# Small tiles moved and padded so that every matmul operand in SBUF begins at a multiple of 512 bytes

## The chip, the core and the metric

The kernel runs on one core of one Trainium2 chip. The metric is the device time of one execution in microseconds (us), as the median of several runs. The profile is of one further execution. TensorE is the matmul engine, VectorE, ScalarE and GpSimd are the others; in the profile they are PE (PEld for its weight loads), DVE, ACT and POOL. SBUF is the on-chip memory: 128 partitions, and a tile has the same address range in each of them. An address below is the byte offset in a partition.

## What is computed

Linear attention with a decaying state for 4 batches, 8 heads, 768 steps and head size 64, and behind it two MLPs over the 3072 tokens:

```python
state = gamma * state + k[t] (outer) v[t];  y[t] = scale * q[t] @ state     # per batch and head
h = x @ w_in;  solu = h * softmax(h);  ln = (solu - mu) / sqrt(var + 1e-6) * g_ln
x = ln @ w_out                                # first MLP, 512 -> 1024 -> 512
h = x @ w_in2;  g = h * cos(h);  out = g @ w_out2       # second MLP, 512 -> 2048 -> 512
```

## The kernel before

**Precision.** Each operand of the MLP matmuls is split in a high and a low half (`split`, line 119: ScalarE writes the high half, VectorE the rest), and each product is three matmuls: high by high, high by low, low by high. Before each matmul TensorE loads its stationary operand (`lhsT`, 128x128); the moving operand (`rhs`) then streams through, 512 columns or, in `mm2`, 256.

**Stages.** The order of TensorE's work is the program's own (a manual schedule); the other engines follow an order that the framework plans from it. Up to about 110 us attention steps, the first MLP and the loading of weights start up. Up to about 380 us 24 attention steps (`att_scores`, `att_state`, `att_out`) alternate with the first MLP: `mm1` (line 284) multiplies 128 tokens by `w_in`, `norm` (line 292 to 305) does the softmax and the normalization with a small tile `sm` of row statistics, `transp` (line 320) transposes, and `mm2` (line 337) multiplies by `w_out`. Then the second MLP goes over six blocks of 512 tokens. Its weights `w2h`, `w2l` are in four chunks of 512 hidden units. For each of 16 groups j of 128 hidden units `up` (line 362) makes 12 matmuls with chunk j // 4; ScalarE and VectorE form h cos(h) (line 369 to 374: a range reduction and a sine with the bias tile `hp`, which holds pi/2, then `split`), and `down` (line 387), three groups later, makes 12 matmuls with `o2h`, `o2l`. So `up` and `down` alternate every 12 matmuls, except that at the beginning of each block after the first the four `up` with chunk 0 follow one another, and at the end of a block 48 of `down` do.

**Where the tiles lie.** SBUF pools grow from two sides: "left" from the low addresses and "right" from the high ones. On the left come, in order: 16,384 bytes for DMA and four constants of 32 bytes each (the program's own, up to 16,512), then `mg` (2048), `cs` (576), `gcol` (32), `mhalf` (4, rounded to 32), `ident` (512), the weights of the first MLP, `u`, `x32`, `xh`, `xl`; then three buffers of `sm` (40 bytes, rounded to 64, each), `junk`, `ys`, and behind them `o1h`, `o1l` and the transposed tiles. On the right, from 229,344 downwards: `w2l`, `w2h` of chunk 0, the staging tiles, and the pool of the attention or, later, of the second MLP, at whose low end `hp` lies (4 bytes, rounded to 32, at 151,488) and above it `yh` at 151,520. Where matmuls are concerned this gives, with every slice that a matmul takes a multiple of 512 bytes from the start of its tile:

| operands | side | start of the first tile | remainder modulo 512 |
|---|---|---|---|
| `ident`, `u` (transposes) | left | 19,200 and 52,480 | 256 |
| `w1h`, `w1l` (moving in `mm1`) | left | 19,712 | 256 |
| `xh`, `xl` (stationary in `mm1`) | left | 89,344 | 256 |
| `o1h`, `o1l` (stationary in `mm2`) | left | 101,824 | 448 |
| `lth`, `ltl` (moving in `mm2`) | left | 134,592 | 448 |
| `w2h`, `w2l`, chunk 0 (stationary in `up`) | right | 212,960 | 480 |
| `w2h`, `w2l`, chunks 1 to 3 (stationary in `up`) | left | 19,712 and 85,248 | 256 |
| `yh`, `yl` (moving in `up`) | right | 151,520 | 480 |
| `gh`, `gl` (stationary in `down`) | right | 180,192 | 480 |
| `o2h`, `o2l` (moving in `down`) | left | 52,480 | 256 |
| tiles of the attention (`X`, `kt`, `W`, `kn`) | right | 157,664 | 480 |

Of the kernel before, what the change touches and what calls it, by code (L numbers as in the profile page):

```python
# [11 lines left out]
F32 = mybir.dt.float32  # L12
# [3 lines left out]
AF = mybir.ActivationFunctionType  # L16
# [28 lines left out]
HALFPI = math.pi / 2.0  # L45
# [5 lines left out]
def body(ctx: ExitStack, tc: tile.TileContext, qx, kt, kn, vn, c_sc, c_mg,  # L51
         w_in1, w_out1, gln, w_in2, w_out2, out):
    nc = tc.nc
# [2 lines left out]

    const = ctx.enter_context(tc.tile_pool(name="const", bufs=1, side="left"))
    dram = ctx.enter_context(tc.tile_pool(name="dram", bufs=1, space=DRAM))
    p_w2a = ctx.enter_context(tc.tile_pool(name="w2a", bufs=1, side="right"))
    stg = ctx.enter_context(tc.tile_pool(name="stg", bufs=2, side="right"))  # L60

# [6 lines left out]
    moe = ph1.enter_context(tc.tile_pool(name="moe", bufs=1, side="left", reuse_waits="tile"))  # L68
# [12 lines left out]
    def load_step(n):  # L81
        bp, i = steps[n]
        d = {}
        d["kt"] = pa.tile([128, 8, C], F32, tag="kt", name="kt", bufs=2)
        d["X"] = pa.tile([128, 2, 8, C], F32, tag="X", name="X")
        d["kn"] = pa.tile([128, NHP, 2 * D], F32, tag="kn", name="kn")
        d["W"] = pa.tile([128, 2, 8, D], F32, tag="W", name="W")
        d["mg"] = pa.tile([128, 2, NHP, C], F32, tag="mg", name="mg", bufs=2)
        nc.sync.dma_start(out=d["kt"], in_=kt[bp, i].rearrange("p (j s) -> p j s", s=C))
        src = qx[bp, i].rearrange("p (j s) -> p j s", s=C)  # L90
        nc.sync.dma_start(out=d["X"][64:128, 0], in_=src[64:128])
        nc.sync.dma_start(out=d["X"][0:64, 1], in_=src[0:64])
        src = vn[bp, i].rearrange("p (j s) -> p j s", s=D)
        nc.sync.dma_start(out=d["W"][0:64, 0], in_=src[0:64])
        nc.sync.dma_start(out=d["W"][64:128, 1], in_=src[64:128])
        nc.sync.dma_start(out=d["kn"], in_=kn[bp, i].rearrange("p (j s) -> p j s", s=2 * D))
        if i == 0:
            nc.gpsimd.memset(d["W"][64:128, 0], 0.0)
            nc.gpsimd.memset(d["W"][0:64, 1], 0.0)
        st[n] = d  # L100
# [7 lines left out]
    nc.scalar.dma_start(out=gcol, in_=gln)  # L108
    mhalf = const.tile([128, 1], F32, name="mhalf")
    nc.gpsimd.memset(mhalf, -0.5)  # L110
    ident = const.tile([128, 128], F32, name="ident")
    make_identity(nc, ident)

# [5 lines left out]
    def split(hi, lo, src, pin=False, head=None):  # L119
        op = nc.scalar.activation(out=hi, in_=src if head is None else head, func=AF.Copy)  # L120
        if pin:
            tc.keep_in_program_order(op)
        nc.vector.tensor_tensor(out=lo, in0=src, in1=hi.bitcast(F32), op=ALU.subtract)  # L123

    p2 = {}
# [85 lines left out]
    def att_prep(n):  # L211
        bp, i = steps[n]
        d = st[n]
        nc.gpsimd.tensor_tensor(out=d["mg"], in0=mg, in1=cs[:, 0:2, i].unsqueeze(3).to_broadcast([128, 2, NHP, C]),
                                op=ALU.mult)
        if i + 1 < NI:
            for a in range(NHP):
                nc.scalar.activation(out=d["kn"][:, a], in_=d["kn"][:, a], func=AF.Copy, scale=cs[:, 2, i, a:a + 1])  # L218
# [13 lines left out]
    def att_state(n):  # L232
        bp, i = steps[n]
        if i + 1 >= NI:
            return
        d, nd = st[n], st[n + 1]
        if i == 0:
            s_ps[0] = psa.tile([128, 8, D], F32, tag="S", name="S")
        sp = s_ps[0]
        k3 = d["kn"].rearrange("p a (b d) -> p (a b) d", b=2)  # L240
        for j in range(8):
            nc.tensor.matmul(out=sp[64:128, j], lhsT=k3[0:64, j], rhs=d["W"][0:64, 0, j],  # L242
                             start=(i == 0 and j == 0), stop=(i == NI - 2 and j == 7), skip_group_check=True)
            nc.tensor.matmul(out=sp[0:64, j], lhsT=k3[64:128, j], rhs=d["W"][64:128, 1, j],  # L244
                             start=(i == 0 and j == 0), stop=(i == NI - 2 and j == 7), skip_group_check=True)
        nc.scalar.activation(out=nd["W"][64:128, 0], in_=sp[64:128], func=AF.Copy)
        nc.scalar.activation(out=nd["W"][0:64, 1], in_=sp[0:64], func=AF.Copy)
# [38 lines left out]

    def norm(n):
        h = hs.pop(n)
        sm = moe.tile([128, 10], F32, tag="sm", name="sm", bufs=3)
        junk = moe.tile([128, 2, 512], BF16, tag="junk", name="junk")  # L290
        u = p_u.tile([128, 2, 512], F32, tag="u", name="u")
        nc.vector.tensor_reduce(out=sm[:, 0:1], in_=h, axis=AX.XY, op=ALU.max, negate=True)
        nc.scalar.activation(out=u, in_=h, func=AF.Exp, bias=sm[:, 0:1], accum_out=sm[:, 1:2])
        nc.vector.scalar_tensor_tensor(out=u, in0=u, scalar=1.0, in1=h, op0=ALU.mult, op1=ALU.mult,
                                       accum_out=sm[:, 2:3])
        nc.vector.tensor_scalar(out=sm[:, 3:4], in0=sm[:, 2:3], scalar1=-1.0 / FF1, scalar2=None, op0=ALU.mult)
        nc.scalar.activation(out=junk, in_=u, func=AF.Square, bias=sm[:, 3:4], accum_out=sm[:, 4:5])
        nc.vector.tensor_scalar(out=sm[:, 5:6], in0=sm[:, 1:2], scalar1=1e-9, scalar2=None, op0=ALU.add)
        nc.vector.scalar_tensor_tensor(out=sm[:, 6:7], in0=sm[:, 5:6], scalar=1e-6, in1=sm[:, 5:6],
                                       op0=ALU.mult, op1=ALU.mult)  # L300
        nc.vector.scalar_tensor_tensor(out=sm[:, 7:8], in0=sm[:, 4:5], scalar=1.0 / FF1, in1=sm[:, 6:7],
                                       op0=ALU.mult, op1=ALU.add)
        nc.gpsimd.tensor_tensor(out=sm[:, 8:9], in0=sm[:, 7:8], in1=mhalf, op=ALU.pow)
        nc.vector.tensor_tensor(out=sm[:, 9:10], in0=sm[:, 3:4], in1=sm[:, 8:9], op=ALU.mult)
        nc.scalar.activation(out=u, in_=u, func=AF.Identity, scale=sm[:, 8:9], bias=sm[:, 9:10])
        lns[n] = u
# [47 lines left out]
    def up(n, j):  # L354
        yh, yl = p2["y", n]
        wh, wl = w2h[j // 4], w2l[j // 4]
        cs = slice((j % 4) * 128, (j % 4) * 128 + 128)
        h = p2["psh"].tile([128, 512], F32, tag="h2", name="h2")
        m = 0
        for k in range(KD):  # L360
            for w, a in ((wh, yh), (wl, yh), (wh, yl)):
                nc.tensor.matmul(out=h, lhsT=w[:, k, cs], rhs=a[:, k], start=(m == 0), stop=(m == 3 * KD - 1))  # L362
                m += 1
        sb = p2["sb"]
        ki = sb.tile([128, 512], I32, tag="ki", name="ki", bufs=2)
        r = sb.tile([128, 512], F32, tag="r", name="r", bufs=2)
        gh = sb.tile([128, 512], F32R, tag="gh", name="gh", bufs=LAG + 1)
        gl = sb.tile([128, 512], F32R, tag="gl", name="gl", bufs=LAG + 1)
        nc.scalar.activation(out=ki, in_=h, func=AF.Identity, scale=INV2PI, bias=0.25)  # L369
        nc.vector.scalar_tensor_tensor(out=r, in0=ki, scalar=-C1, in1=h, op0=ALU.mult, op1=ALU.add)  # L370
        nc.vector.scalar_tensor_tensor(out=r, in0=ki, scalar=-C2, in1=r, op0=ALU.mult, op1=ALU.add)
        nc.vector.tensor_scalar(out=r, in0=r, scalar1=HI, scalar2=LO, op0=ALU.min, op1=ALU.max)  # L372
        nc.scalar.activation(out=r, in_=r, func=AF.Sin, bias=p2["hp"])  # L373
        nc.vector.tensor_tensor(out=r, in0=r, in1=h, op=ALU.mult)  # L374
        split(gh, gl, r)
        p2["g", n, j] = (gh, gl)
# [49 lines left out]
    def attend():  # L426
        n = nxt[0]
        if n >= ns:
            return
        nxt[0] += 1  # L430
        if 4 < n + 2 < ns:
            load_step(n + 2)
        if n == 0:
            att_state(n)
            att_out(n)
        if n + 1 < ns:
            att_prep(n + 1)
            att_scores(n + 1)
        if n > 0:
            att_state(n)  # L440
            att_out(n)
        if n == ns - 1:
            att.close()
            p2["psh"] = ctx.enter_context(tc.tile_pool(name="psh", bufs=3, side="right", space=PSUM, reuse_waits="tile"))
            p2["sb"] = ctx.enter_context(tc.tile_pool(name="sb2", bufs=1, side="right", reuse_waits="tile"))
            p2["hp"] = p2["sb"].tile([128, 1], F32, name="hp")
            nc.gpsimd.memset(p2["hp"], HALFPI)

    def first(n, c):
        if c == 1 and 0 < n < 2 * NG - 1:  # L450
# [183 lines left out]
```

## Time and profile before

| | |
|---|---|
| median of 3 runs | 952.97 us (952.46 to 953.57) |
| the profiled execution | 950.22 us |
| its span, first to last instruction | 948.4 us |
| TensorE matmuls busy | 917.0 us (97%) |
| TensorE weight loads busy | 776.5 us (82%) |
| VectorE, ScalarE, GpSimd busy | 622.4, 452.8, 47.8 us |

The span is what the trace covers; the time of an execution has 1.8 us around it. Matmuls are pipelined: the recorded length of one overlaps the next, so busy time says only that TensorE had work. How fast that goes is seen from the starts in the timeline, or from the chain of waits, in which each piece of several instructions stands with its length.

### The profile page before, as it was taken

Reading aid. Unit: us, or ns where it says so; the run is one execution under the profiler, and the core shown is the slowest. Engines: PE = TensorE matmul, PEld = TensorE weight load, DVE = VectorE, ACT = ScalarE, POOL = GpSimd, SP = SyncE. Lnnn points to the kernel's source line nnn. Section 1 sums busy time; section 2 is a strip of 40 time slices with the busy share of each in tenths; the row PEclk is TensorE's granted clock in tenths of the full one; section 3 lists DMA queues with packets and bytes.
Section 4 is the critical chain, followed back from the end, with each engine's and each line's share of the span. In section 5 each row is a group of like instructions: output and inputs, shape, how many; then the busy total and the mean of one; then the engine's idle time right before and its main releaser. Section 6 shows DMA issues by size and latency. Waiting matters only on the chain.

```text
span 948.4 us, 16045 instructions
## 1 busy us (share of the span) xinstructions
PE 917.0 (97%) x6464; PEld 776.5 (82%) x6464; DVE 622.4 (66%) x1090; ACT 452.8 (48%) x768; POOL 47.8 (5%) x60
## 2 busy tenths in 40 slices
PE   4887999999999999999999999999999999999997
PEld 4676899899898999998888888888888888888886
DVE  5899887668677664566657555755665566556553
ACT  4677756565655544644434333433433343334332
POOL 2112110110101100000000000000000000000000
PEclk9999999999999999999999999999999999999999
DMA  9997355656456332242011003000300020001001
GB/s 257 283 257 201 113 153 170 197 168 216 154 170 204 105 101 67 83 145 73 1 53 37 0 1 90 1 1 0 89 1 1 23 66 1 1 23 45 0 1 45
DMA packets 41882, 85.26 MB, mean 90 GB/s; under 512 B 5456, under 2 KB 11728, under 8 KB 41808
## 3 DMA queue, kind: packets, MB, share of 16 engines
q1 hardware_dynamic: 41376, 83.91, 29.9%
q8 instruction: 50, 0.82, 0.4%
q10 hardware_dynamic: 432, 0.34, 0.1%
q14 instruction: 24, 0.20, 0.1%
HBM read 64.30 MB, written 19.92 MB: 89 GB/s over the span
## 4 chain that ended last, share of the span: by engine, by line
PE 90%; DMA 4%; DVE 2%; ACT 2%; issue 1%; SPq 0%; POOL 0%; ACTq 0%; DVEq 0%
PE acc L387 28%; PE h L362 28%; PE y L337 14%; PE h L284 11%; DMA kn<-kn_dram 3%; PE tr L320 2%; PE y L256 2%; PE sc L224 2%; PE S L244 1%; DMA W<-vn_dram 1%; DVE X L227 1%; ACT kn L218 1%; DMA mg<-c_mg_dram 0%; PE S L242 0%; PE sc L225 0%
## 5 line engine op out<-in xcount | busy, mean ns | idle before, releaser
L387 PE MATMUL acc<-o2h,gl 128*128 128x512 f32 x384 | 151.9, 396 | 0.0
L387 PE MATMUL acc<-o2l,gh 128*128 128x512 f32 x384 | 151.8, 395 | 0.0
L362 PE MATMUL h<-yh,w2h 128*128 128x512 f32 x384 | 151.8, 395 | 0.0
L362 PE MATMUL h<-yl,w2h 128*128 128x512 f32 x384 | 151.5, 395 | 0.0
L362 PE MATMUL h<-yh,w2l 128*128 128x512 f32 x384 | 151.5, 395 | 0.0
L387 PE MATMUL acc<-o2h,gh 128*128 128x512 f32 x384 | 151.5, 395 | 0.0
L373 ACT ACTIVATE r<-r,hp 128x512 f32<-128x512 f32 x96 | 69.3, 722 | 144.9 <-DVE r L372 144.6
L370 DVE SCALAR_TENSOR_TENSOR r<-ki,h 128x512 f32<-128x512 int32 x96 | 66.0, 687 | 73.7 <-ACT ki L369 72.6
L337 PE MATMUL y<-lth,o1h 128*128 128x256 f32 x384 | 110.4, 287 | 0.0
L337 PE MATMUL y<-ltl,o1h 128*128 128x256 f32 x384 | 108.9, 284 | 0.0
L337 PE MATMUL y<-lth,o1l 128*128 128x256 f32 x384 | 108.7, 283 | 0.0
L374 DVE TENSOR_TENSOR r<-r,h 128x512 f32<-128x512 f32 x96 | 66.0, 688 | 61.6 <-ACT r L373 61.6
L369 ACT ACTIVATE ki<-h 128x512 int32<-128x512 f32 x96 | 57.2, 596 | 85.6 <-PE h L362 84.8
L123 DVE TENSOR_TENSOR gl<-r,gh 128x512 fp32r<-128x512 f32 x96 | 66.3, 691 | 45.9 <-ACT gh L120 45.4
L120 ACT ACTIVATE gh<-r 128x512 fp32r<-128x512 f32 x96 | 60.6, 632 | 65.0 <-DVE r L374 64.9
L387 PEld LDWEIGHTS acc<-o2h,gl 128*128 128x128 f32 x384 | 72.1, 188 | 17.7
L387 PEld LDWEIGHTS acc<-o2h,gh 128*128 128x128 f32 x384 | 72.0, 188 | 17.4
L387 PEld LDWEIGHTS acc<-o2l,gh 128*128 128x128 f32 x384 | 72.1, 188 | 17.2
L362 PEld LDWEIGHTS h<-yl,w2h 128*128 128x128 f32 x384 | 72.2, 188 | 17.0
L362 PEld LDWEIGHTS h<-yh,w2h 128*128 128x128 f32 x384 | 72.2, 188 | 16.9
L362 PEld LDWEIGHTS h<-yh,w2l 128*128 128x128 f32 x384 | 72.2, 188 | 16.6
L284 PE MATMUL h<-w1h,xh 128*128 128x512 f32 x192 | 77.8, 405 | 0.0
(79 smaller groups left out, 1597.3 us busy)
## 6 DMA issues: line engine op xcount, KB each, us to landing
raw<-w_in_dram SPq DMA_DIRECT2D x24, 512.0 KB, 4.6
raw<-w_out_dram SPq DMA_DIRECT2D x24, 512.0 KB, 4.4
kt<-kt_dram SPq DMA_DIRECT2D x24, 256.0 KB, 4.6
X<-qx_dram SPq DMA_DIRECT2D x48, 128.0 KB, 4.9
W<-vn_dram SPq DMA_DIRECT2D x48, 128.0 KB, 4.5
kn<-kn_dram SPq DMA_DIRECT2D x24, 256.0 KB, 4.8
y1d<-ys SPq DMA_DIRECT2D x24, 256.0 KB, 2.2
yt<-y1d SPq DMA_DIRECT2D x24, 256.0 KB, 3.0
```

What stands on the lines that cost most here:

```text
L120: op = nc.scalar.activation(out=hi, in_=src if head is None else head, func=AF.Copy)
L123: nc.vector.tensor_tensor(out=lo, in0=src, in1=hi.bitcast(F32), op=ALU.subtract)
L224: nc.tensor.matmul(out=sc[0:64, j], lhsT=d["kt"][64:128, j], rhs=d["X"][64:128, 0, j], start=True, stop=True)
L256: nc.tensor.matmul(out=y[64 * par:64 * par + 64, j], lhsT=d["W"][:, par, j], rhs=d["X"][:, par, j], start=True, stop=True)
L284: nc.tensor.matmul(out=h[:, c], lhsT=a[:, k], rhs=w[:, k, cs], start=(k + m == 0), stop=(k == KD - 1 and m == 2))
L337: nc.tensor.matmul(out=y1[:, e], lhsT=w[:, j, ds], rhs=a[:, j % 2], start=(m == 0), stop=(m == 3 * K1 - 1))
L362: nc.tensor.matmul(out=h, lhsT=w[:, k, cs], rhs=a[:, k], start=(m == 0), stop=(m == 3 * KD - 1))
L369: nc.scalar.activation(out=ki, in_=h, func=AF.Identity, scale=INV2PI, bias=0.25)
L370: nc.vector.scalar_tensor_tensor(out=r, in0=ki, scalar=-C1, in1=h, op0=ALU.mult, op1=ALU.add)
L373: nc.scalar.activation(out=r, in_=r, func=AF.Sin, bias=p2["hp"])
L374: nc.vector.tensor_tensor(out=r, in0=r, in1=h, op=ALU.mult)
L387: nc.tensor.matmul(out=acc, lhsT=a[:, ts_], rhs=w, start=(j == 0 and m == 0), stop=(j == K2 - 1 and m == 2))
```

## The change

A new pool on the right, opened before all others of that side, holds `hp` as a tile of 480 bytes, of which the first element is set to pi/2 at the start of the program and read by the sine; before, `hp` was a tile of 4 bytes in the pool of the second MLP, set when the attention was done. The row statistics `sm` are now three tiles of 64 bytes among the constants on the left, taken in turn by `n % 3`, ahead of `ident`, with a `pad` of 64 bytes behind them; before, they were three buffers of a pool, behind `xl`. No arithmetic and no instruction on data changes, and no operand changes its side.

```diff
--- before.py
+++ after.py
@@ -56,6 +56,8 @@
 
     const = ctx.enter_context(tc.tile_pool(name="const", bufs=1, side="left"))
     dram = ctx.enter_context(tc.tile_pool(name="dram", bufs=1, space=DRAM))
+    p_hp = ctx.enter_context(tc.tile_pool(name="hp", bufs=1, side="right"))
+    hp = p_hp.tile([128, 120], F32, name="hp")
     p_w2a = ctx.enter_context(tc.tile_pool(name="w2a", bufs=1, side="right"))
     stg = ctx.enter_context(tc.tile_pool(name="stg", bufs=2, side="right"))
 
@@ -108,6 +110,9 @@
     nc.scalar.dma_start(out=gcol, in_=gln)
     mhalf = const.tile([128, 1], F32, name="mhalf")
     nc.gpsimd.memset(mhalf, -0.5)
+    nc.gpsimd.memset(hp[:, 0:1], HALFPI)
+    sms = [const.tile([128, 16], F32, name=f"sm{n}") for n in range(3)]
+    const.tile([128, 16], F32, name="pad")
     ident = const.tile([128, 128], F32, name="ident")
     make_identity(nc, ident)
 
@@ -286,7 +291,7 @@
 
     def norm(n):
         h = hs.pop(n)
-        sm = moe.tile([128, 10], F32, tag="sm", name="sm", bufs=3)
+        sm = sms[n % 3]
         junk = moe.tile([128, 2, 512], BF16, tag="junk", name="junk")
         u = p_u.tile([128, 2, 512], F32, tag="u", name="u")
         nc.vector.tensor_reduce(out=sm[:, 0:1], in_=h, axis=AX.XY, op=ALU.max, negate=True)
@@ -370,7 +375,7 @@
         nc.vector.scalar_tensor_tensor(out=r, in0=ki, scalar=-C1, in1=h, op0=ALU.mult, op1=ALU.add)
         nc.vector.scalar_tensor_tensor(out=r, in0=ki, scalar=-C2, in1=r, op0=ALU.mult, op1=ALU.add)
         nc.vector.tensor_scalar(out=r, in0=r, scalar1=HI, scalar2=LO, op0=ALU.min, op1=ALU.max)
-        nc.scalar.activation(out=r, in_=r, func=AF.Sin, bias=p2["hp"])
+        nc.scalar.activation(out=r, in_=r, func=AF.Sin, bias=hp[:, 0:1])
         nc.vector.tensor_tensor(out=r, in0=r, in1=h, op=ALU.mult)
         split(gh, gl, r)
         p2["g", n, j] = (gh, gl)
@@ -443,8 +448,6 @@
             att.close()
             p2["psh"] = ctx.enter_context(tc.tile_pool(name="psh", bufs=3, side="right", space=PSUM, reuse_waits="tile"))
             p2["sb"] = ctx.enter_context(tc.tile_pool(name="sb2", bufs=1, side="right", reuse_waits="tile"))
-            p2["hp"] = p2["sb"].tile([128, 1], F32, name="hp")
-            nc.gpsimd.memset(p2["hp"], HALFPI)
 
     def first(n, c):
         if c == 1 and 0 < n < 2 * NG - 1:
```

## Rows read from the trace of the kernel before

**Rows 1.** The profile's page: part 1, busy time of the engines.

```profile
PE 917.0 (97%) x6464; PEld 776.5 (82%) x6464; DVE 622.4 (66%) x1090; ACT 452.8 (48%) x768; POOL 47.8 (5%) x60
```

**Rows 2.** The cores: span and mean granted TensorE clock.

```profile
core 0: 948.4 us, clock 0.993
```

**Rows 3.** Windows by stage; the first line names the columns.

```profile
core 0: us, PE busy (x) PEld busy (x) DVE busy (x) ACT busy (x) POOL busy (x), PEclk, DMA share, GB/s
0.00:25.00 25.00, 12.60 (x193) 11.41 (x194) 14.65 (x25) 10.90 (x23) 5.10 (x12) 1.00 0.91 262
25.00:50.00 25.00, 19.03 (x292) 15.61 (x290) 20.56 (x35) 14.38 (x31) 2.45 (x2) 0.93 1.03 290
...
240.00:380.00 140.00, 139.81 (x1316) 126.65 (x1315) 90.04 (x184) 75.55 (x125) 11.10 (x15) 1.00 0.41 132
490.00:580.00 90.00, 90.00 (x389) 72.69 (x388) 54.53 (x89) 35.46 (x58) 0.00 (x0) 1.00 0.09 24
```

**Rows 4.** TensorE's waits, the longest: total us, times, longest one.

```profile
PE sc L224 <- DMA X<-qx_dram: 11.1, 2, 5.7
```

**Rows 5.** The chain of waits, second MLP: start us, length us, what.

```profile
485.87 11.20 PE acc L387 x48
497.07 10.92 PE h L362 x48
...
516.38 2.80 PE h L362 x12
```

**Rows 6.** Timeline of TensorE, `up` with chunk 0: matmuls 1, 10; then `down`.

```profile
496.90 0.40 PE L362 MATMUL h<-yh,w2h 128*128 128x512 f32 x1
...
498.98 0.39 PE L362 MATMUL h<-yh,w2h 128*128 128x512 f32 x1
...
507.82 0.40 PE L387 MATMUL acc<-o2h,gh 128*128 128x512 f32 x1
```

**Rows 7.** Timeline of TensorE, `mm1` after `mm2`: matmuls 1, 10, 24.

```profile
110.53 0.39 PE L284 MATMUL h<-w1h,xh 128*128 128x512 f32 x1
...
112.62 0.39 PE L284 MATMUL h<-w1h,xh 128*128 128x512 f32 x1
...
115.79 0.39 PE L284 MATMUL h<-w1l,xh 128*128 128x512 f32 x1
```

**Rows 8.** Timeline, matmul and next weight load: `down`, then `up` with chunk 0.

```profile
486.17 0.40 PE L387 MATMUL acc<-o2l,gh 128*128 128x512 f32 x1
486.18 0.19 PEld L387 LDWEIGHTS acc<-o2h,gh 128*128 128x128 f32 x1
...
500.34 0.39 PE L362 MATMUL h<-yh,w2h 128*128 128x512 f32 x1
500.35 0.19 PEld L362 LDWEIGHTS h<-yh,w2l 128*128 128x128 f32 x1
```

**Rows 9.** Timeline of TensorE, `down` after `mm2`: matmuls 1, 3, 10, 12.

```profile
418.53 0.39 PE L387 MATMUL acc<-o2h,gh 128*128 128x512 f32 x1
...
418.98 0.39 PE L387 MATMUL acc<-o2l,gh 128*128 128x512 f32 x1
...
420.61 0.40 PE L387 MATMUL acc<-o2h,gh 128*128 128x512 f32 x1
...
421.08 0.39 PE L387 MATMUL acc<-o2l,gh 128*128 128x512 f32 x1
```

**Rows 10.** Groups by shape, one of each three: count, busy us, mean ns.

```profile
L387 PE MATMUL acc<-o2h,gl 128*128 128x512 f32 x384 | 151.9, 396 | 0.0
...
L362 PE MATMUL h<-yh,w2h 128*128 128x512 f32 x384 | 151.8, 395 | 0.0
...
L284 PE MATMUL h<-w1h,xh 128*128 128x512 f32 x192 | 77.8, 405 | 0.0
```

**Rows 11.** The chain of waits, mixed stage, `mm2`.

```profile
146.07 5.75 PE y L337 x48
```

**Rows 12.** Tile `hp`: its memset (min/median/max ns, first and last start).

```profile
L447 POOL MEMSET hp<- x1: 103/103/103, 343.3 to 343.3; 128x1 f32 x1
```

## The prediction, made before the change was run

> **What bounds the kernel now.** I read the busy times of the engines, the clock, the windows by stage, TensorE's waits, and then the chain and the timeline inside two stages. TensorE is busy for 917.0 us [rows 1] of the span's 948.4, at a mean granted clock of 0.993 [rows 2], so nearly all of it at the 2.4 GHz level. By stage [rows 3]: from 490 to 580 us, inside the second MLP, TensorE is busy for all 90 us at clock 1.00, with VectorE at 54.5 us and ScalarE at 35.5 us; from 240 to 380 us, in the mixed stage, it is busy for 139.8 of 140. Its idle time lies at the start, where it is busy for 12.6 and 19.0 us of the first two stretches of 25; the longest wait is for X from DRAM, 11.1 us in total [rows 4]. So after about 100 us the time is a number of matmuls times the distance from one start to the next, which I call the pitch. The recorded length of a matmul (395 ns) is not that: matmuls overlap, and the pitch is read from the chain and the timeline.
>
> The pitch of the 128x512 matmuls has two values. In the chain [rows 5], 48 matmuls of `down` take 11.20 us, 233.3 ns each, and 12 of `up` take 2.80 us, 233.3 ns each; but 48 of `up` with the first weight chunk take 10.92 us. In the timeline of those 48 [rows 6] the first nine need 498.98 - 496.90 = 2.08 us (231 ns each), and the other 39 need 507.82 - 498.98 = 8.84 us, 226.7 ns each. `mm1` does the same [rows 7]: nine at (112.62 - 110.53) / 9 = 232 ns, then fourteen at (115.79 - 112.62) / 14 = 226.4 ns.
>
> Beside the start addresses of the operands (the table above), this sorts itself. Where moving and stationary operand have the same remainder modulo 512 (`mm1` 256 and 256, `up` with chunk 0 480 and 480), the pitch settles at 226.7. Where the remainders differ (`down` 256 and 480, `up` with chunks 1 to 3 480 and 256) it never does: the 48 of `down` in a row stay at 233.3. Length of the run is therefore not the reason. Work in between is not either: the weight load of the next matmul starts within 10 ns of the running one in both cases and takes 0.19 us [rows 8], so both reads run side by side. And the pitch takes some matmuls to change: `down` after `mm2` (448 and 448) starts at 418.98 - 418.53 = 0.45 us for two, and some matmuls on needs 0.47 us for two (421.08 - 420.61) [rows 9].
>
> **The change, part by part.** The left side moves up by 192 bytes of row statistics and 64 of padding, so everything from `ident` to `xl` goes from remainder 256 to 0. Behind `xl` the three old statistics tiles are gone, so `o1`, `lt` and what lies there move by 256 - 192 = 64 bytes, from 448 to 0. The right side moves down by 480 bytes, from 480 to 0. All pairs then have the same remainder, and that is the whole of the expected effect.
>
> The terms, from the counts in [rows 10]:
> - `down`: 3 x 384 = 1152 matmuls, from 233.3 to 226.7 ns: 6.6 x 1152 = 7.6 us.
> - `up`: 1152 matmuls, of which three chunks in four, 864, have unlike remainders: 6.6 x 864 = 5.7 us.
> - `up` with chunk 0: the slow start of its 48 goes, 10.92 - 48 x 0.2267 = 0.04 us, in five blocks of tokens: 0.2 us.
> - `mm1`: 19 runs of 12 or 24 follow `mm2` with another remainder (448, then 256), as in [rows 7], and each pays 9 x (232 - 226.4) = 0.05 us. With one remainder throughout this may go (0.9 us) or not (0). I take 0.5.
> - `mm2`: 48 take 5.75 us [rows 11], 119.8 ns for 256 columns, with like remainders already: 0.
>
> The sum is 14.0 us. No other engine takes the place of TensorE: in 490 to 580 us VectorE is busy for 61% [rows 3], and 14 us of 530 us make that 62%. In `up`'s chain of ScalarE and VectorE steps nothing is waited for by TensorE now [rows 4], and `down` trails `up` by three, which leaves some 17 us for it (3 x 5.6, from [rows 5]).
>
> The moved small tiles cost nothing. The memset of `hp` takes 103 ns at 343.3 us, in the middle of the mixed stage [rows 12]; it goes to the start, on GpSimd, ahead of `ident`, which no one needs before the first transposes. The cover there is the wait for the first operands (11.1 us [rows 4]); without it the memset would cost its 0.1 us. The three statistics tiles rotate by n modulo 3 as the pool's buffers did, so each write waits for the same readers three tiles back; that they are one allocation each from the start removes a wait at most. DMAs: the count and sizes are unchanged, but all tiles on the right that DMAs fill now start at another remainder. The trace has no pair of like DMAs that differ only in that, so the price is unknown. In the first 50 us the DMA engines are busy for 0.91 and 1.03 of the time [rows 3], and there it would show. As bounds I take 1 us of gain and 1 us of loss, an estimate: a tenth of the 11.1 us of waiting for X [rows 4]. I count 0, the middle, since no row speaks for either end.
>
> The profiled execution took 950.22 us, 2.75 us under the median of the runs. Its span would go from 948.4 to 934.4, it to 936.2, and the median from 952.97 to **939.0 us**.
>
> **A rule against the change.** The rows say that a like remainder is worth 6.6 ns of pitch. The Trainium skill, TensorE: Matmul & The Clock Gate, "Step-by-step: what each phase is for", says that the moving operand and the weight load each have a read port of their own, so that loading weights takes no read bandwidth from the running matmul. By that rule the sum is 0 and the time stays at 952.97 us; the trace agrees that the two overlap, and disagrees on the pitch, unless something other than the remainder tells the two groups apart. That is the second rival.
>
> **The rivals.**
> 1. *The slow start returns at every switch* (chance 0.20). `up` and `down` alternate every 12 matmuls, in about 156 runs (2304 / 12 = 192, less those that stand together as 48). If each switch costs nine slow matmuls as in [rows 6, 7], that is 156 x 0.05 = 7.8 us of the 14.0, leaving 6.2: 946.8 us. For it: every slow start in the trace is at a switch. Against it: all of these switches also change the remainder, the step from one `up` to the next inside the 48 costs nothing [rows 6], and `down` after `mm2` begins fast [rows 9].
> 2. *It is the side of SBUF, not the remainder* (0.10). All pairs with like remainders lie on one side, and all with unlike ones take one operand from each side; the change moves no operand across. Then nothing in `up` and `down` changes: 952.97 us, within 0.2%. Against it: `mm1`'s slow start [rows 7] has both operands on the left, as has the `mm2` before it, and only the remainder is new.
> 3. *Remainder 0 is a worse place to be alike in* (0.06). The pitch settles at a value that like remainders set; 256 and 480 give 226.7, but 0 has not been tried. If both reads beginning on the same boundary collide, the 2304 + 576 = 2880 wide matmuls could settle one step of 6.6 ns above 233.3 instead of below: 2304 x 6.6 + 576 x 13.2 = 22.8 us more, 976 us. It decides as soon as the settled pitch passes 233.3 ns. Against it: 256 and 480 give the same 226.7, so the value of the common remainder has made no difference so far.
> 4. *More than 14 us* (0.03): the pitch falls under 226.7. 256 columns more cost 226.7 - 119.8 = 107 ns, so some 13 ns of each matmul are not columns, and without them 30 us would go. No row is lower than 226.
>
> That the change doesn't do what it says I leave out: the tile sizes add up as above on both sides.
>
> **How the numbers follow.** The forecast has 0.61. Its own range is 936 to 942, from the terms of `mm1` and the DMAs (0.5 and 1 us either way) and the scatter of the runs. To hold 8 in 10 the range reaches to rival 1, and leaves out rivals 2, 3 and 4 (0.19): 935.5 to 947.5 us. A measurement of this kernel tells about 0.2% (1.9 us) from no change. Faster: 0.61 + 0.20 + 0.03 = 0.84; the same: 0.10; slower: 0.06.
>
> **What would show it.** In the chain of the changed kernel 48 of `down` should take 10.88 us in place of 11.20, and 12 of `up` or `down` 2.72 in place of 2.80. `mm1` after `mm2` should begin at 227 rather than 232. TensorE should keep its idle time at the start and gain none after 420 us. Rival 1 would show 2.77 for 12 and 10.92 for 48; rival 2 2.80 for 12 of either; rival 3 more than 2.80. The forecast is wrong if the pitch is right but TensorE waits in the second MLP, or if the first 100 us move by more than 1 us.

## The result and the profile after

The changed kernel takes 936.25 us, the median of 6 runs (934.7 to 938.93), against 952.37 us for the kernel before in the same comparison (950.14 to 953.57, 6 runs). The ratio is 0.9838, with a 95% interval from 0.9819 to 0.9858: 1.6% faster. The profiled execution took 935.94 us, with a span of 934.2 us where it was 948.4.

The span is 14.2 us shorter, and TensorE's busy time falls by about as much, 14.6 us: 917.0 us [rows 1] became 902.4. The same number of matmuls is in both. The other engines have the busy times that they had, within 0.7 us. From the profile's page, part 1:

```profile
PE 902.4 (97%) x6464; PEld 776.1 (83%) x6464; DVE 623.1 (67%) x1090; ACT 452.7 (48%) x768; POOL 47.8 (5%) x60
```

The chain of waits shows where it went. Its columns are the start in us, the length in us, and what ran. First the second MLP, the stretch that answers to [rows 5]:

```profile
480.55 2.72 PE h L367 x12
483.27 10.88 PE acc L392 x48
494.15 10.88 PE h L367 x48
505.03 2.72 PE acc L392 x12
507.75 2.72 PE h L367 x12
```

In place of 11.20 us for 48 of `down` stands 10.88, in place of 2.80 for 12 stands 2.72, and the 48 of `up` with chunk 0 lost their slow start as well, 10.92 to 10.88. Each of these is 226.7 ns per matmul. `up` and `down` follow each other without a slow matmul in between: the switch itself costs nothing here.

Then the mixed stage of the same chain:

```profile
110.92 5.47 PE h L289 x24
...
124.49 2.75 PE h L289 x12
...
146.24 5.75 PE y L342 x48
```

Here little has changed: `mm2` takes the 5.75 us of [rows 11], and 24 of `mm1` take 5.47 us. In the timeline of TensorE, `mm1` after `mm2` still begins slowly (start us, recorded length us, engine, line, operation, operands):

```profile
110.76 0.40 PE L289 MATMUL h<-w1h,xh 128*128 128x512 f32 x1
...
111.92 0.39 PE L289 MATMUL h<-w1l,xh 128*128 128x512 f32 x1
112.15 0.39 PE L289 MATMUL h<-w1h,xh 128*128 128x512 f32 x1
112.37 0.39 PE L289 MATMUL h<-w1h,xl 128*128 128x512 f32 x1
```

The first five need 111.92 - 110.76 = 1.16 us, 232 ns each, and from then on the pitch (the distance from one start to the next) is 0.22 to 0.23 us. Before the change nine were slow [rows 7].

The span falls into two parts at the first `down`. It starts here:

```profile
417.80 0.40 PE L392 MATMUL acc<-o2h,gh 128*128 128x512 f32 x1
```

From there to the end are 934.2 - 417.8 = 516.4 us. Before, it was 948.4 - 418.5 = 529.9 us [rows 9]. So 13.5 us come from the second MLP and 0.7 us from all that stands ahead of it. Inside the second MLP TensorE is still busy all the time, in the columns of [rows 3]:

```profile
490.00:580.00 90.00, 90.00 (x399) 74.55 (x398) 55.23 (x90) 34.90 (x58) 0.00 (x0) 1.00 0.10 29
```

The longest of TensorE's waits is still the one for X at the start, as in [rows 4]:

```profile
PE sc L229 <- DMA X<-qx_dram: 12.7, 2, 7.2
```

### The profile page after: what moved, and what is told of

It reads as the page before. It is cut to its first block, busy times and chain, and to the rows that moved or that the text cites. A ratio compares the mean times of both kernels' runs of the same rounds, so it can differ in the third digit from the quotient of the medians.

```text
span 934.2 us, 16044 instructions
## 1 busy us (share of the span) xinstructions
PE 902.4 (97%) x6464; PEld 776.1 (83%) x6464; DVE 623.1 (67%) x1090; ACT 452.7 (48%) x768; POOL 47.8 (5%) x60
## 4 chain that ended last, share of the span: by engine, by line
PE 89%; DMA 5%; DVE 2%; SPq 1%; ACT 1%; issue 1%; ACTq 0%; DVEq 0%
PE h L367 28%; PE acc L392 28%; PE y L342 15%; PE h L289 12%; PE tr L325 2%; PE y L261 2%; PE sc L229 1%; DMA raw<-w_out_dram 1%; DMA kt<-kt_dram 1%; PE S L249 1%; DMA X<-qx_dram 1%; DMA kn<-kn_dram 1%; DVE X L232 1%; SPq L138 1%; DMA W<-vn_dram 0%
## 5 line engine op out<-in xcount | busy, mean ns | idle before, releaser
L367 PE MATMUL h<-yh,w2h 128*128 128x512 f32 x384 | 149.6, 390 | 0.0
L367 PE MATMUL h<-yl,w2h 128*128 128x512 f32 x384 | 149.4, 389 | 0.0
L367 PE MATMUL h<-yh,w2l 128*128 128x512 f32 x384 | 149.4, 389 | 0.0
L392 PE MATMUL acc<-o2h,gh 128*128 128x512 f32 x384 | 149.4, 389 | 0.0
L392 PE MATMUL acc<-o2h,gl 128*128 128x512 f32 x384 | 149.4, 389 | 0.0
L392 PE MATMUL acc<-o2l,gh 128*128 128x512 f32 x384 | 149.4, 389 | 0.0
```

Source lines behind the costliest of these rows:

```text
L392: nc.tensor.matmul(out=acc, lhsT=a[:, ts_], rhs=w, start=(j == 0 and m == 0), stop=(j == K2 - 1 and m == 2))
```

## The experiments

The prediction's theory was that a pair of operands with the same remainder modulo 512 settles at 226.7 ns, wherever it lies. The rivals were the side of SBUF and the multiple of 512 itself. Twelve runs were made, in three groups; three of them repeat a kernel, so that there are nine new ones. A kernel with one execution is read from its chain, not from its time; why that is safer is shown at the end of this section.

**Both sides at 256, none at a multiple of 512 (e1).** Against the kernel before; the left side stays as it was:

```diff
+    p_hp = ctx.enter_context(tc.tile_pool(name="hp", bufs=1, side="right"))
+    hp = p_hp.tile([128, 56], F32, name="hp")
...
+    nc.gpsimd.memset(hp[:, 0:1], HALFPI)
...
-        nc.scalar.activation(out=r, in_=r, func=AF.Sin, bias=p2["hp"])
+        nc.scalar.activation(out=r, in_=r, func=AF.Sin, bias=hp[:, 0:1])
...
-            p2["hp"] = p2["sb"].tile([128, 1], F32, name="hp")
-            nc.gpsimd.memset(p2["hp"], HALFPI)
```

> Only the right side moves, by 224 bytes, so that both sides have the remainder 256: no operand of the second MLP begins at a multiple of 512, but all of its pairs are alike. Theory (like remainders count, whatever they are): 12 matmuls of up or down take 2.72 us in the chain and 48 take 10.88, as in the changed kernel, and the time is 936 us, within 2. Rival (the multiple of 512 itself counts): 2.80 and 11.20, and 952 us as before.

Measured: 939.93 us (936.79 to 943.93, 4 runs), ratio 0.9879 (0.9834 to 0.9923). The chain of its second MLP:

```profile
484.00 2.72 PE h L365 x12
486.72 10.88 PE acc L390 x48
497.60 10.88 PE h L365 x48
508.48 2.72 PE acc L390 x12
```

The pitch is that of the changed kernel to the last digit, with no operand of the second MLP on a multiple of 512. The multiple itself is not what counts. The time is 2 us above the expected range's end. In the profile that lies ahead of the second MLP: the first `down` starts 3.4 us later than in the changed kernel, and from there to the end both take 516.4 us. How much this part scatters is shown below.

```profile
421.23 0.39 PE L390 MATMUL acc<-o2h,gh 128*128 128x512 f32 x1
```

**The right side alone, to 0 (e2).** As e1, with a larger tile:

```diff
-    hp = p_hp.tile([128, 56], F32, name="hp")
+    hp = p_hp.tile([128, 120], F32, name="hp")
```

> Only the right side moves, by 480 bytes, to remainder 0; the left stays at 256. Theory: up with chunk 0 is alike (0 and 0) and settles at 226.7 ns, up with chunks 1 to 3 and down are unlike (0 and 256) and stay near 233.3: 2.80 us for 12, span 948 us, within 2. Rival (each operand at a multiple of 512 helps by itself): half the way, 2.76 us for 12 and about 941 us.

Measured: 939.16 us, span 937.4. Neither expectation held. `down` now pairs 0 with 256, which by the theory is unlike, and yet:

```profile
483.76 2.72 PE h L365 x12
486.48 10.88 PE acc L390 x48
497.36 10.88 PE h L365 x48
```

A difference of 256 bytes is as good as none. The theory's modulus was too large.

**The left side alone, to 0 (e3).** Against the kernel before, the three statistics tiles and the pad, without `hp`:

```diff
+    sms = [const.tile([128, 16], F32, name=f"sm{n}") for n in range(3)]
+    const.tile([128, 16], F32, name="pad")
...
-        sm = moe.tile([128, 10], F32, tag="sm", name="sm", bufs=3)
+        sm = sms[n % 3]
```

> Only the left side moves, to remainder 0; the right stays at 480, so the pairs of the second MLP differ by 32 bytes alone. Theory with a strict rule (remainders must be equal): 2.80 us for 12, span 948 us. Theory with a coarse rule (a small difference is as good as none): 2.72 us for 12 and 934 us. Rival (each side by itself): half the way, about 941 us.

Measured: 950.92 us, span 949.1.

```profile
483.75 2.80 PE h L364 x12
486.56 11.20 PE acc L389 x48
497.75 10.92 PE h L364 x48
```

Nothing is gained in the second MLP. The remainders there are 480 and 0, which is a distance of 32 bytes, so a small distance is not as good as none. After e2 this run also says less than it seemed to: modulo 256 the pairs stand as they stood in the kernel before (480 leaves 224, and 256 and 0 both leave 0). This part of the change, the move of the statistics, does nothing for `up` and `down` by itself.

**`mm1` unlike by 256, on one side (e4).** As e1, with a padding ahead of `x32`:

```diff
     moe = ph1.enter_context(tc.tile_pool(name="moe", bufs=1, side="left", reuse_waits="tile"))
+    moe.tile([128, 64], F32, name="mpad")
```

> As the kernel with both sides at 256, with 256 bytes of padding before x32, so that in mm1 alone the stationary operand (0) and the moving one (256) are unlike, both on the left side. Theory: mm1 never settles, 24 of its matmuls take 5.60 us in the chain instead of 5.48, and the span is 2 to 3 us longer than that of the kernel with both sides at 256; up and down stay at 2.72 us for 12. Rival (operands on different sides of SBUF are what is slow): mm1 stays at 5.48 us for 24 and the span does not change.

Measured: 939.31 us, span 937.5. 24 of `mm1` stay at 5.48 us:

```profile
169.36 5.48 PE h L288 x24
```

This was meant to tell the side of SBUF from the remainder, and it doesn't. The theory as recorded expected 5.60 and missed; after e2 a difference of 256 counts as like, so both theories give 5.48. The run does confirm e2 for another pair of tiles, both on the left.

**Differences of 64 and of 128 (e5, e6).** The changed kernel with `hp` of 416 and of 352 bytes, which puts the right side at 64 and at 128 while the left is at 0:

```diff
-    hp = p_hp.tile([128, 120], F32, name="hp")
+    hp = p_hp.tile([128, 104], F32, name="hp")     # e5; 88 in e6
```

> The changed kernel with a tile hp of 416 bytes: the right side is at remainder 64, the left at 0. So far a difference of 256 acts as none, and differences of 32 and 224 act as unlike; both of the bad ones are odd multiples of 32. Theory A (the step is 64 bytes): 2.72 us for 12 matmuls of up or down, span as in the changed kernel within 4 us. Theory B (the step is 128 or 256 bytes): 2.80 us for 12, second MLP 13.6 us longer, span about 948 to 951 us.

> The same with hp of 352 bytes: right side at 128, left at 0. Theory A (step of 64) and a step of 128: 2.72 us for 12. Theory B with a step of 256: 2.80 us for 12.

Measured: 950.13 us for e5 and 949.49 for e6. The chains, e5 first:

```profile
481.48 2.80 PE acc L392 x12
484.28 2.76 PE h L367 x12
487.04 11.20 PE acc L392 x48
498.24 10.90 PE h L367 x48
```

```profile
482.61 2.80 PE h L367 x12
485.41 11.20 PE acc L392 x48
496.61 10.89 PE h L367 x48
```

Both are unlike. In e5 `up` with chunks 1 to 3 comes to 2.76 in a part of the groups, between the two values, and `down` doesn't; why is open. So differences of 0 and 256 are good, and 32, 64, 128 and 224 (the kernel before: 480 against 256) are not: a step of 256 bytes fits every run. Other multiples of 32, such as 96 and 160, were not tried, and differences under 32 bytes were not, as tiles are placed in steps of 32.

**One weight load of three unlike (e7).** As e1, with `hp` of 192 bytes (the right side at 288) and 32 bytes of padding below `gl`, so that everything of the second MLP below it returns to 256. Unlike are then `gl` and the weights of chunk 0:

```diff
-    hp = p_hp.tile([128, 56], F32, name="hp")
+    hp = p_hp.tile([128, 48], F32, name="hp")
...
+        if "gpad" not in p2:
+            p2["gpad"] = sb.tile([128, 8], F32, name="gpad")
         gl = sb.tile([128, 512], F32R, tag="gl", name="gl", bufs=LAG + 1)
```

> Both sides alike by 256, except gl and the first weight chunk, which are off by 32 bytes: of the three stationary operands of down one, gl, is unlike (a third of its 1152 matmuls), up with chunks 1 to 3 is alike, up with chunk 0 is unlike throughout. Theory (each weight load pays by itself when it is unlike the moving operand beside it): down gains two thirds, 12 take about 2.75 us, 48 take 10.99, and up of chunk 0 takes 11.20 for 48. Rival (one unlike load in three keeps the stream from settling): down stays at 2.80 for 12 and 11.20 for 48. Both: up of chunks 1 to 3 between 2.72 and 2.80, as it settles anew after each 12 of down or not.

Measured: 950.0 us, span 948.2.

```profile
483.48 2.80 PE acc L392 x12
486.27 2.72 PE h L365 x12
489.00 11.20 PE acc L392 x48
500.19 11.20 PE h L365 x48
```

This is the most telling picture of the study, because good and bad stand side by side. `down`, with `gl`, the stationary operand of one matmul in three, off by 32 bytes, has the whole loss, 11.20 for 48: it is not a price per unlike load. The `up` groups between them, all alike, are at 2.72 at once. And the 48 of `up` with chunk 0, whose operands both lie on the right, are at 11.20, where they settled in every other kernel. So the side of SBUF is not the cause: one side can be slow (here), and a pair across the sides can be fast (the changed kernel).

**`mm2` unlike by 32 (e8).** As e2, with a padding ahead of `lth`; the stationary operand of `mm2` is at 448, the moving one at 480:

```diff
     p2["lt"] = ph1.enter_context(tc.tile_pool(name="lt", bufs=1, side="left", reuse_waits="tile"))
+    p2["lt"].tile([128, 8], F32, name="lpad")
```

> Only the right side moved (to 0), with 32 bytes of padding before lth, so that in mm2 alone the stationary operand (448) and the moving one (480) differ by 32, both on the left side. Theory: mm2, which now settles at 120 ns, no longer does; if an unlike pair costs it what it costs the wide matmuls (6.6 ns), 48 take 6.06 us in place of 5.75, and 24 such runs add 7.6 us. Rival (the matmul of 256 columns settles at a slower pitch than it begins with, 116 to 118 ns, and unlike operands keep it there): 48 take 5.65 us and 2 to 3 us are gained. Rival (it takes operands on two sides of SBUF): 5.75, no change.

Measured: 936.62 us, span 934.4.

```profile
148.50 5.61 PE y L340 x48
164.42 5.80 PE y L340 x48
170.23 5.45 PE h L287 x24
```

The matmuls of 256 columns become faster when they are unlike: 5.61 us for 48 in place of 5.75, 116.9 ns each in place of 119.8. The price that the theory gave for an unlike pair has the wrong sign here, and the first rival of this run is right.

**Timed together (e9 to e12).** The changed kernel once more (e9), e2 once more (e10), e8 once more (e11), and the changed kernel with `hp` of 224 bytes and the padding of e8 (e12), all beside the same runs of the kernel before (951.63 us, 949.67 to 953.91, 11 runs).

> The changed kernel once more, beside the three kernels that follow. All theories: 936 us, within 2.

> Only the right side moved, by 480 bytes. Theory (pairs must be equal modulo 256, and the left was so already): the whole gain in the second MLP, 13.5 us, and at most 0.5 us less than the changed kernel in mm1, whose slow start after mm2 is nine matmuls here and five there: 936.5 us, within 2. Rival (the move of the left side is worth more than its slow starts): 938 us or more.

> Only the right side moved, and lt lies 32 bytes past its place, so that mm2 is unlike. In one profile mm2 took 3.1 us less in all. Theory: 3 us less than the kernel with the right side alone, 933.5 us, within 2. Rival (the gain of mm2 is taken back by slower starts or waits around it): no difference, 936.5 us.

> The changed kernel with hp of 224 bytes (right side at 256) and lt 32 bytes past its place: wide matmuls alike modulo 256, mm2 unlike. Theory: up and down 2.72 us for 12, mm2 5.61 to 5.80 for 48, 3 us less than the changed kernel: 933 us, within 2. Rival (as for the kernel before this): 936 us.

| kernel | median, us | lowest to highest | ratio to before (95% interval) |
|---|---|---|---|
| e9, the changed kernel | 936.46 | 933.81 to 937.42 | 0.9836 (0.9814 to 0.9857) |
| e10, right side alone | 937.46 | 935.95 to 943.48 | 0.9861 (0.9835 to 0.9887) |
| e11, right side, `mm2` unlike | 935.50 | 934.50 to 936.42 | 0.9830 (0.9811 to 0.9849) |
| e12, both sides, `mm2` unlike | 936.08 | 932.54 to 938.51 | 0.9834 (0.9811 to 0.9856) |

The intervals overlap, so times alone order none of the four. Their second MLPs are alike, and in e11 and e12 `mm2` keeps its gain in the chain; e11 first:

```profile
145.15 5.61 PE y L340 x48
```

```profile
144.16 5.60 PE y L342 x48
160.10 5.80 PE y L342 x48
```

Over all 1152 matmuls of `mm2` the distances from one start to the next add up to 140.1 us in e9 and e10, 136.9 in e11 and 137.0 in e12, so 3.1 us less work of TensorE. But the medians differ by 2.0 us (e10 to e11) and 0.4 us (e9 to e12), within their scatter. The 3 us that the theory expected did not show in full in the times: e11 lies 2.0 us above its forecast, between theory and rival, and e12 3.1 us, where the rival had it. In the traces the stage of `mm2` itself is shorter: from the first `mm2` to the first `down` it is 311.1 us in e8, 313.0 in e11 and 311.1 in e12, against 312.9 to 315.7 in the eleven traces with like operands. Whether the unlike `mm2` makes the whole kernel faster is therefore open.

Where the scatter comes from can be read from two starts, that of the first `mm2` and that of the first `down`. In e12's and in e7's profile they are

```profile
103.19 0.38 PE L342 MATMUL y<-lth,o1h 128*128 128x256 f32 x1
...
414.28 0.39 PE L392 MATMUL acc<-o2h,gh 128*128 128x512 f32 x1
```

```profile
107.01 0.39 PE L340 MATMUL y<-lth,o1h 128*128 128x256 f32 x1
...
422.59 0.40 PE L392 MATMUL acc<-o2h,gh 128*128 128x512 f32 x1
```

The first `down` starts 8.3 us later in e7. Of that, 3.8 us are there before the first `mm2`, and 4.5 us arise behind it, 3.1 of them in `mm2`. In the first part TensorE waits for DMAs, and not equally long in every execution. Its wait for X (total us, times, longest one) is, for e12 and then e7:

```profile
PE sc L229 <- DMA X<-qx_dram: 10.7, 2, 5.8
```

```profile
PE sc L227 <- DMA X<-qx_dram: 13.6, 2, 7.9
```

So from one execution the span can mislead by several us. The pitch of the second MLP repeats: where the same kernel was profiled twice (the changed kernel and e9, e2 and e10), groups of 12 take 2.72 us and of 48 take 10.88 or 10.89, but for one of 10.99 in e9.

## Why the prediction was right, and where it was not

**The bound** held: the second MLP is a count of matmuls times their pitch, and nothing else came up when the pitch fell: TensorE is busy for 90.00 of the 90 us from 490 to 580, and VectorE for 55.2 of them (61%, where 62% was expected).

**The terms of `up` and `down`** held: 7.6 + 5.7 + 0.2 = 13.5 us were forecast, and 13.5 us is what the stretch from the first `down` to the end lost. The settled pitch of 226.7 ns, read from the few stretches before the change in which operands were alike, was the pitch of `up` and `down` after it. The exceptions are the few groups of 12 that stand between or right behind runs of `mm2`; they take 2.75 us.

**The term of `mm1`** was forecast at 0.5 us, between 0 and 0.9, on the ground that a like remainder might remove the slow start after `mm2`. It removed a part: 12 matmuls fell from 2.77 to 2.75 us in the chain, and 24 from 5.48 to 5.47, so over 19 such runs it is 0.2 to 0.4 us. The sign set for it, a beginning at 227, did not come: the first five still need 232 ns each. It was the left half of the change that did this much, as e3 has 2.75 and 5.47 too and e2 still 2.77 and 5.48. The reason given, that a slow start comes from a change of the remainder, was incomplete: there is one also where all remainders are 0 and only the columns step from 256 to 512. That step does not settle it either: behind the unlike `mm2` of e8 the same 24 matmuls take 5.44 to 5.50 us in the chain, and 5.44 is 226.7 ns each, with hardly a slow start. What sets its length stays open.

**The DMAs and the small tiles** were counted at 0, within 1 us either way. The first `mm2` starts 0.2 us later than before, well under the 1 us at which the forecast was to be called wrong (before, then after):

```profile
104.68 0.39 PE L337 MATMUL y<-lth,o1h 128*128 128x256 f32 x1
```

```profile
104.91 0.39 PE L342 MATMUL y<-lth,o1h 128*128 128x256 f32 x1
```

All that stands ahead of the first `down` became 0.7 us shorter in the profile, `mm1` included. Both are less than that part scatters, so that the price was near 0 is not shown beyond a few us.

**The time** was forecast as 939.0 us against a median of 952.97, a gain of 14.0 us. The profile gained 14.2 us. The medians gave 16.1 us, whose interval, 1.42% to 1.81% of 952.37 us, is 13.5 to 17.2 us. The sum of the terms is thus borne out by the profile. The median is 2.7 us under the forecast, and that it is still inside the stated range, by 0.75 us, is in part luck: the forecast added 2.75 us because the profiled execution before lay that far under the median, and after the change this distance is 0.3 us (935.94 against 936.25).

**The rule against the change** was that a weight load takes no read bandwidth from the running matmul (the Trainium skill, TensorE: Matmul & The Clock Gate, "Step-by-step: what each phase is for"). The time that the prediction drew from it, no change, did not come. In e1 and e7 the arithmetic is the same and only the places of tiles differ, by 32 bytes, and the 48 of `down` take 10.88 us in one and 11.20 in the other. The overlap of the two reads is there in both: the weight load, 0.19 us long, starts within 10 ns of the running matmul. That these two reads are what disturbs each other is not shown.

**The rule of the prediction was too narrow.** It said modulo 512; the runs show modulo 256 (e2, e4). It was right for this kernel because the change brings all operands of the two MLPs to one remainder, which satisfies either. It also means that for the second MLP half of the change was not needed: the kernel before had the left side at 256 already, and a right side moved by 224 or 480 bytes has the whole gain there (e1, e2). The other half gives the second MLP nothing (e3). Whether it gives the whole kernel anything is open: the intervals of e9 and e10 overlap, but from the first `mm2` to the first `down` the two traces of the changed kernel take 312.9 and 313.7 us and those of e1, e2 and e10 take 314.7 to 315.7. One group of matmuls is not at a multiple of 512 even after the change: those of the attention take slices of 256 bytes, so that every second slice begins at an odd multiple of 256. Modulo 256 their pairs were alike before and after, and in the mixed stage they take 37.3 us in both kernels.

**The rivals.** The slow start at every switch (0.20) fell: `up` and `down` alternate at 2.72. The side of SBUF (0.10) fell by the changed kernel and by e7. Remainder 0 as a worse place (0.06) fell: 0 and 256 give the same 226.7. A settled pitch under 226.7 (0.03) was not seen in any kernel at 512 columns.

## What to carry to other kernels

Where TensorE is the bound, divide the length of a long run in the chain by its count, for each kind of matmul, and lay the start addresses of both operands beside it: two values for one shape, with no wait between, can come from placement. In this kernel 512-column matmuls in 32-bit types took 2.9% less time when moving and stationary operands started at the same place modulo 256 bytes, and one stationary operand of three off by 32 bytes was enough to lose it, so a tile of 4 bytes at the edge of a pool is worth a look at what it shifts. At 256 columns the sign was the other way, at the one difference of 32 bytes that was tried, so the pitch should be measured for each shape.

## What was not expected of the hardware

Like and unlike operands differ in kind, not just in size. Alike, 256 columns take 119.8 ns (5.75 us / 48) and 512 take 226.7, so 256 more columns cost 106.9 ns and 13 ns are left over for each matmul. Unlike, 256 columns take 116.9 ns (5.61 / 48) and 512 take 233.3, so 256 more cost 116.4 ns and hardly anything is left over. Read as two straight lines, an unlike pair pays by the column and a like pair once for each matmul, and so the first is better at 256 columns and the second at 512. With two widths only, that it is a line is not shown. If it is, the two would meet near 335 columns, an estimate from these four numbers that no run tests. Which accesses stand in each other's way was not observed: the runs show the distance of the two start addresses and its effect, and nothing of the memory in between.
